# Another order for weight conversions, sums and copies in an attention and two-layer kernel

## The chip, the core and the metric

The kernel runs on one core of one Trainium2 chip. The time is that of the whole program on the device in microseconds (us). PE is TensorE (matrix products), DVE is VectorE, ACT is ScalarE, POOL is GpSimd, SP is SyncE, which here only issues DMAs. Every engine works through its own queue in order: an instruction that waits holds up all that stand behind it on that engine.

## The reference

```python
# attention with a decay per head, for 2 sequences of 768, 8 heads of 64
for t in range(S):
    state = gamma[None, :, None, None] * state + np.einsum('bhd,bhe->bhde', k[:, :, t], v[:, :, t])
    y[:, :, t] = scale * np.einsum('bhd,bhde->bhe', q[:, :, t], state)
...
x = np.ascontiguousarray(attn_out.transpose(0, 2, 1, 3)).reshape(B * S, H * D)   # 1536 x 512
...
return (a * b @ w_out)      # a = x @ w_a, b = x @ w_b; d_ff 1536: the first layer, gives y
...
h = x @ w_in                # the second layer, x is y; d_ff 2048
g = np.maximum(0.01 * h, h)
return (g @ w_out)
```

## The kernel before

**Numbers.** Every product runs with two-part operands: a value is rounded to a short form, `hi`, by ACT, and the rest, `lo`, is the difference, taken by DVE (`split`). A product is three matmuls, hi·hi, hi·lo and lo·hi (`mm3`, L249 to L251). The weights come from HBM in 64 bits a number (`raw`). They are brought to 32 bits, which the code calls rounding: `begin_weights` issues three ACT instructions (absolute value, low bits, sign) and `round_steps` three DVE instructions (L309, L311, L315). Then a weight is split like any other operand.

**Stages on PE.** Attention runs 0 to 47 us in 12 units `u` (256-column pieces of scores, states and outputs). The first layer follows in 12 blocks of `d_ff`, f = 0 to 11, to 246 us: `a` and `b` are products of x with weight blocks a_f and b_f, their product is h[t, f] for the three 512-token tiles t. From f = 3 to 10 (`fast`) the block uses sums of x made beforehand (`mixed_items`: eight DVE sums `xf`, L675, and eight splits s, L683) to save products. Then comes y's stage, 248 to 326 us: h times w_out by Strassen's scheme of seven products, each over six j (class `Seven`; its n = 6 to 41 here, `blk` in the trace, one product of 2.1 us for each n, in the order p7, p2, p6, p5, p4, p3). For every n it makes operand forms (`forma`): an ACT cast and a DVE difference for each part of h and w_out. They are prepared four products ahead (`LEAD1`). The second layer's h2 = y · w_in follows with f = 0 to 15 (326 to 490 us), with the products `blk<-form` of its own w_out in between, and its tail runs to 580 us.

**What sets the order.** The order on every engine is the order in which the code is run. A list `queue` holds small items with a cost in us; `pump(us)` runs items while PE's work of that length is emitted. `enqueue_round` and `enqueue_split` put a weight's rounding and split on it; two tables, `PARK` and `WITH`, say which further weights are rounded in which f: `WITH` the blocks of w_out (wo), `PARK` first blocks of the second layer's wi and wq, which are stored to HBM (L321, POOL's queue) and fetched again.

**Space.** SBUF has 81 slots of 128x512 numbers. A new tile takes the slot that was given back longest ago, and waits for the last user of it. Of h's blocks 18 (`AWAY`) are sent to HBM as soon as they are made (`send`, L650, POOL's queue) and brought back (`bring`, L660, SP's queue). The sums of h that the seven products need are accumulating DMAs in POOL's queue (L127); some read the sent block in HBM. For a brought block h[2, f] with f < 6 `bring` also issues an accumulating DMA (L662), an add-back, which waits for the bring.

Of the kernel before, what the change touches and what calls it, by code (L numbers as in the profile page):

```python
# [14 lines left out]
U32 = mybir.dt.uint32  # L15
I64 = mybir.dt.int64
ALU = mybir.AluOpType
# [17 lines left out]
LATE = 8  # L35
STEPS = {6: 1, 7: 1, 8: 1, 9: 1, 10: 1}
NWARM = 10
# [4 lines left out]
LEAD1 = 4  # L42
PARK = (0, 0, 0, 0, 0, 0, 0, 0, 0, 0, 1, 2)
WITH = ((), (), (), (0,), (1,), (2,), (3,), (4,), (5,), (6, 7), (8, 9), (10, 11))
MADE = ((), (), (), (), (0,), (1,), (2,), (3,), (4,), (5,), (), ())
# [176 lines left out]
def retention_moe_kernel(ctx: ExitStack, tc: tile.TileContext, ins, out):  # L222
# [61 lines left out]

    def begin_weights():

        n = at["begin"]
        key = order[n]
        raw = raws[key]
        u = slots.new(F32, f"{key[0]}{key[1]}")  # L290
        low = tmp.tile([P, TT], I32, tag="low", name=f"low{n}")
        nc.scalar.activation(u, word(raw, F32, 1), AF.Abs, scale=2.0 ** -112)
        nc.scalar.mul(low, word(raw, U32, 0), 2.0 ** -29)
        sign = signs[n % len(signs)]
        nc.scalar.mul(word16(sign, F16, 1), word(raw, F32, 1), 2.0 ** -100)
        begun[key] = (u, low, sign)
        at["begin"] += 1
# [61 lines left out]
    def enqueue_split(key, keep=False):  # L359
# [4 lines left out]
        def low():  # L364
            src = rounded.pop(key)
            if key[0] == "a":
                nc.scalar.mul(weights[key][1], as32(weights[key][0]), -1.0)
                nc.gpsimd.dma_start(weights[key][1], src, accum_op=ALU.add)
            else:
                nc.vector.tensor_sub(weights[key][1], src, as32(weights[key][0]))  # L370
            if keep:
                kept[key] = src
            else:
                slots.done(1)

        behind.extend([(0.05, high), (0.05 if key[0] == "a" else 0.61, low)])

# [265 lines left out]

    far = {}

# [8 lines left out]
    def bring(reserve=0):  # L654

        for key in list(far)[:1]:
# [4 lines left out]
            if key[0] == 2 and key[1] < FF1 // 2:  # L661
                nc.gpsimd.dma_start(h[key], h[2, key[1] + FF1 // 2], accum_op=ALU.add)  # L662

# [136 lines left out]
    for i in range(2):  # L800
        signs.append(tmp.tile([P, TT], I32, tag=f"sign{i}", name=f"sign{i}", bufs=1))
        nc.gpsimd.memset(signs[i], 0)
    warm = ap.tile([P, TT], BF16, tag="warm", name="warm")
# [15 lines left out]
    def first_weights():  # L819
        begin_weights()  # L820
        yield
        yield from round_steps()
        yield
        want("a", 0)
# [3 lines left out]
    for u in range(-1, len(units)):  # L828
# [21 lines left out]
        if u < 0:  # L850
            prep(2)
        else:
            prep(u + 3)
        loads(u + 8)
        if u + 8 == 7 or u + 8 >= len(units):
# [17 lines left out]
    for t in range(NTILE):  # L873
        if t < 2:
            want("ab"[t], 1)
        pbs.append(bank(f"pb{t}0"))
        ab_mm(pbs[t], t, 0, 1, range(KC))
# [28 lines left out]
    for f in range(1, FF1):  # L906
        if f + 1 < FF1:
            for k in "ab":
                enqueue_round()
                enqueue_split((k, f + 1), f + 1 in FAST)  # L910
        for n in MADE[f][:1]:
# [74 lines left out]
    for n in range(NMADE, len(z.plan) - 2):  # L986
        bring(8)
        if n == NMADE:
            bring(8)
        z.prep(n + LEAD1)  # L990
        if n >= 3 * H1:
# [9 lines left out]
        if n == 6 * H1 - LEAD1:  # L1001
            slots.done(H1)
        if n in (5 * H1, 6 * H1 - 2):
            want("wi", int(n != 5 * H1))
# [75 lines left out]
    for f in range(FF2):  # L1080
# [4 lines left out]
        for n, step in enumerate(steps):  # L1085
# [4 lines left out]
            if n == 0 and f == FF2 - 1:  # L1090
                keep(z, u2, "p1")
            if n == 0 and f >= HALF:
                z.prep(f)
            if n == (f > 0):
                if f + 1 < FF2:
# [91 lines left out]
```

## Time and profile before

| what | value |
|---|---|
| median of 3 runs | 582.33 us (581.12 to 582.61) |
| the profiled execution | 582.3 us, of which 580.4 us are the span of instructions |
| busy: PE, DVE, ACT, POOL | 570.8, 448.0, 374.3, 85.6 us |
| granted TensorE clock | 1.00 of full speed throughout |

The span is what the profile shows from the first to the last instruction; 1.9 us of the execution lie outside it. PE's busy time is 98% of the span, and PE's instructions and their order are the same before and after the change.

### The profile page before, as it was taken

The numbers are of one execution on the slowest core, as the hardware profiler recorded it, in microseconds if no ns is written. First come the engines' busy times: TensorE is split into PE (matmuls) and PEld (weight loads), VectorE is DVE, ScalarE is ACT, GpSimd is POOL, SyncE is SP. The second block draws the span as 40 slices with busy tenths as digits, with TensorE's granted clock in tenths as the row PEclk, the third lists the DMA queues.
The fourth block names the chain that finished last, engine by engine and source line by source line (L and its number), as shares of the span: only waits on it lengthen the run. The fifth ranks groups of instructions, "written<-read, shape, count | busy, mean of one in ns | idle before, by whom it ended". The sixth has DMA issues, their size and how long they took to land.

```text
span 580.4 us, 9183 instructions
## 1 busy us (share of the span) xinstructions
PE 570.8 (98%) x3287; PEld 479.8 (83%) x3287; DVE 448.0 (77%) x899; ACT 374.3 (64%) x778; POOL 85.6 (15%) x107
## 2 busy tenths in 40 slices
PE   9999989999999999999999999999999999999997
PEld 5988878888888887888788878888888888888886
DVE  5886497898897985796799487676887657879992
ACT  4776456776676865784768487767675456688710
POOL 3331300013233211038900000000000000000000
PEclk9999999999999999999999999999999999999999
DMA  8994923557676565699960052433431000010111
GB/s 326 386 365 167 238 86 96 158 140 170 172 209 188 157 204 185 244 331 196 189 139 1 0 182 78 141 108 110 142 98 51 1 0 1 2 55 1 56 54 55
DMA packets 34702, 79.59 MB, mean 137 GB/s; under 512 B 4000, under 2 KB 8352, under 8 KB 34656
## 3 DMA queue, kind: packets, MB, share of 16 engines
q1 hardware_dynamic: 23184, 58.99, 29.7%
q0 software_dynamic: 11184, 19.67, 17.2%
q8 instruction: 26, 0.43, 0.3%
q10 hardware_dynamic: 288, 0.34, 0.2%
q14 instruction: 20, 0.16, 0.1%
HBM read 57.49 MB, written 8.65 MB: 114 GB/s over the span
## 4 chain that ended last, share of the span: by engine, by line
PE 82%; DMA 8%; issue 3%; DVE 3%; ACT 2%; POOL 1%; DVEq 0%; POOLq 0%; ACTq 0%
PE blk L250 10%; PE blk L249 10%; PE blk L251 10%; PE h L251 8%; PE h L249 8%; PE h L250 8%; DMA h<-far 3%; PE sc L503 2%; PE top L249 2%; PE top L250 2%; PE top L251 2%; DMA xf<-x02l 2%; PE pa L251 2%; PE pb L251 2%; PE pb L249 2%
## 5 line engine op out<-in xcount | busy, mean ns | idle before, releaser
L250 PE MATMUL blk<-form,form 128*128 128x512 f32 (+1 forms) x224 | 75.8, 338 | 0.0
L249 PE MATMUL blk<-form,form 128*128 128x512 f32 (+1 forms) x224 | 75.5, 337 | 0.0
L251 PE MATMUL blk<-form,form 128*128 128x512 f32 (+1 forms) x224 | 75.3, 336 | 0.0
L157 DVE TENSOR_TENSOR form<-g,form 128x512 fp32r<-128x512 f32 x112 | 57.2, 551 | 2.4 <-ACT form L151 0.7
L1039 ACT ACTIVATE g<-h 128x512 f32<-128x512 f32 x48 | 28.6, 596 | 46.3 <-PE h L251 46.3
L151 ACT CAST form<-g 128x512 fp32r<-128x512 f32 x112 | 52.7, 514 | 8.5 <-DVE g L132 6.4
L249 PE MATMUL blk<-forma,forma 128*128 128x512 f32 (+1 forms) x168 | 56.8, 338 | 1.0 <-ACT forma L151 1.0
L250 PE MATMUL blk<-forma,forma 128*128 128x512 f32 (+1 forms) x168 | 57.1, 340 | 0.3 <-DVE forma L157 0.2
L251 PE MATMUL blk<-forma,forma 128*128 128x512 f32 (+1 forms) x168 | 56.5, 336 | 0.0
L157 DVE TENSOR_TENSOR forma<-h,forma 128x512 fp32r<-128x512 f32 x84 | 42.9, 550 | 8.7 <-ACT forma L151 8.2
L249 PEld LDWEIGHTS blk<-form,form 128*128 128x128 f32 x224 | 42.5, 190 | 5.5
L250 PEld LDWEIGHTS blk<-form,form 128*128 128x128 f32 x224 | 42.5, 190 | 5.0
L251 PEld LDWEIGHTS blk<-form,form 128*128 128x128 f32 x224 | 42.3, 189 | 4.7
L151 ACT CAST forma<-h 128x512 fp32r<-128x512 f32 x84 | 39.2, 511 | 8.7 <-DMA h<-far 6.6
L127 POOL DMA_DIRECT2D h<-h x34 | 36.2, 1409 | 5.2 <-DVE forma L157 2.7
L157 DVE TENSOR_TENSOR form<-wq,form 128x256 fp32r<-128x256 f32 x56 | 23.5, 419 | 17.1 <-ACT form L151 16.6
L249 PEld LDWEIGHTS blk<-forma,forma 128*128 128x128 f32 x168 | 31.9, 190 | 5.1 <-ACT forma L151 1.2
L250 PEld LDWEIGHTS blk<-forma,forma 128*128 128x128 f32 x168 | 31.8, 190 | 4.5 <-DVE forma L157 0.9
L251 PEld LDWEIGHTS blk<-forma,forma 128*128 128x128 f32 x168 | 31.7, 189 | 3.4
L132 DVE TENSOR_TENSOR g<-g,g 128x512 f32<-128x512 f32 (+1 forms) x56 | 30.6, 570 | 0.5 <-ACT g L1039 0.5
L151 ACT CAST form<-wq 128x256 fp32r<-128x256 f32 x56 | 22.6, 404 | 5.4 <-PE blk L251 2.1
L650 POOL DMA_DIRECT2D far<-h x18 | 10.1, 563 | 89.6 <-DVE h L740 45.0
(3081 smaller groups left out, 1565.9 us busy)
## 6 DMA issues: line engine op xcount, KB each, us to landing
raw_wi<-in_w SPq DMA_DIRECT2D x16, 512.0 KB, 3.4
raw_wq<-in_w SPq DMA_DIRECT2D x16, 512.0 KB, 3.4
raw_a<-in_wab SPq DMA_DIRECT2D x12, 512.0 KB, 5.5
raw_b<-in_wab SPq DMA_DIRECT2D x12, 512.0 KB, 4.0
raw_wo<-in_wo SPq DMA_DIRECT2D x12, 512.0 KB, 5.1
far<-h POOLq DMA_DIRECT2D x18, 256.0 KB, 4.5
h<-far SPq DMA_DIRECT2D x18, 256.0 KB, 6.6
h<-far POOLq DMA_DIRECT2D x13, 256.0 KB, 7.0
```

The lines of the kernel that those rows point to most:

```text
L127: queue.append((0.0, lambda piece=piece: self.nc.gpsimd.dma_start(self.A(*d[1:], j)[piece], self.A(*x1[1:], j)[piece], accum_op=ALU.add)))
L132: queue.append((cost, lambda piece=piece: run(*(self.A(*x[1:], j)[piece] for x in (d, x0, x1)))))
L151: nc.scalar.copy(h, src)
L157: nc.vector.tensor_sub(*todo.pop(0))
L249: nc.tensor.matmul(ps, w[0], x[0], start=first, stop=False, skip_group_check=more)
L250: nc.tensor.matmul(ps, w[0], x[1], start=False, stop=False, skip_group_check=more)
L251: nc.tensor.matmul(ps, w[1], x[0], start=False, stop=last, skip_group_check=more)
L503: nc.tensor.matmul(sc[h][:, c], d["k"][r, c], d["qs"][r, c], start=True, stop=True)
L650: nc.gpsimd.dma_start(far[t, f], h[t, f])
L1039: nc.scalar.activation(g[t, f], ps, AF.Lrelu, alpha=0.01)
```

## The change

It changes order only, with two small exceptions: the `lo` parts of two weights (a2 and a11) are made another way, and one weight less (wi1) is stored and fetched.

- **Third weight blocks.** a2 and b2 are put on the list while f = 0 is still running, ahead of the x sums, where they stood after them before. a2's and a11's `lo` is made by a DVE difference in place of an ACT negation and an accumulating DMA on POOL's queue (L367, L368).
- **Tables.** One stored weight less (wi1), and wo7 is rounded in the list of f = 10 in place of f = 9.
- **h's sums.** The blocks h[2, f] are brought back from n = 12 on, not from n = 6 on, and their three add-backs are issued together at n = 16, behind the 21 sums of p7.
- **w_in roundings.** wi1 and wq1 are rounded in y's stage, on the list of n = 13 and n = 24; wi2 is then split at f = 0, n = 2 of the second layer.
- **Late splits.** For f = 11 to 14 of the second layer the ACT part of the next wi's rounding stands right after the first step's `g`.
- **Begin.** The three ACT instructions of a rounding are ordered absolute, sign, low (before: absolute, low, sign), and for a0 in attention they are spread over units 6 and 7. The two clears of the sign buffers go from POOL's start to units 3 and 4.

```diff
-STEPS = {6: 1, 7: 1, 8: 1, 9: 1, 10: 1}
+STEPS = {6: 2, 7: 2, 8: 1, 9: 1, 10: 1}
...
-PARK = (0, 0, 0, 0, 0, 0, 0, 0, 0, 0, 1, 2)
-WITH = ((), (), (), (0,), (1,), (2,), (3,), (4,), (5,), (6, 7), (8, 9), (10, 11))
+PARK = (0, 0, 0, 0, 0, 0, 0, 0, 0, 0, 0, 2)
+WITH = ((), (), (), (0,), (1,), (2,), (3,), (4,), (5,), (6,), (7, 8, 9), (10, 11))
...
     def begin_weights():
+        for _ in begin_steps():
+            pass
+
+    def begin_steps():
...
         nc.scalar.activation(u, word(raw, F32, 1), AF.Abs, scale=2.0 ** -112)
-        nc.scalar.mul(low, word(raw, U32, 0), 2.0 ** -29)
+        yield
         sign = signs[n % len(signs)]
         nc.scalar.mul(word16(sign, F16, 1), word(raw, F32, 1), 2.0 ** -100)
+        yield
+        nc.scalar.mul(low, word(raw, U32, 0), 2.0 ** -29)
...
-            if key[0] == "a":
+            if key[0] == "a" and keep:
                 nc.scalar.mul(weights[key][1], as32(weights[key][0]), -1.0)
                 nc.gpsimd.dma_start(weights[key][1], src, accum_op=ALU.add)
...
+    def enqueue_next(f):
+        for k in "ab":
+            enqueue_round()
+            enqueue_split((k, f), f in FAST)
...
             if key[0] == 2 and key[1] < FF1 // 2:
-                nc.gpsimd.dma_start(h[key], h[2, key[1] + FF1 // 2], accum_op=ALU.add)
+                back.append(key)
+
+    def add_back():
+        for _, f in back:
+            nc.gpsimd.dma_start(h[2, f], h[2, f + FF1 // 2], accum_op=ALU.add)
+        back.clear()
...
-        nc.gpsimd.memset(signs[i], 0)
...
+        if u in (3, 4):
+            nc.gpsimd.memset(signs[u - 3], 0)
...
     for t in range(NTILE):
         if t < 2:
             want("ab"[t], 1)
+        if t == 1:
+            enqueue_next(2)
+            queue.extend(behind)
+            behind.clear()
...
     for f in range(1, FF1):
-        if f + 1 < FF1:
-            for k in "ab":
-                enqueue_round()
-                enqueue_split((k, f + 1), f + 1 in FAST)
+        if 1 < f < FF1 - 1:
+            enqueue_next(f + 1)
...
     for n in range(NMADE, len(z.plan) - 2):
-        bring(8)
-        if n == NMADE:
+        if n >= 2 * H1:
             bring(8)
+        if n == 3 * H1 - 2:
+            add_back()
...
+        if n in (2 * H1 + 1, 4 * H1):
+            enqueue_round()
...
+            if n == 0 and f >= FF2 - 5 and at["begin"] < min(at["load"], len(order)):
+                begin_weights()
             if n == 0 and f >= HALF:
                 z.prep(f)
+            if f == 0 and n == 2:
+                want("wi", 2)
```

On DVE, where f = 1 begins, this stood before (xf20 is the sum of x for tile 2, part 0; a2_145 the weight a2 in slot 145, and the last number of a name counts tiles):

```order
L675 TENSOR_TENSOR xf22_129_888<-xf20_127_882,xf22_129_888 128x512
L675 TENSOR_TENSOR xf20_127_882<-xf00_131_894,xf20_127_882 128x512
L675 TENSOR_TENSOR xf00_131_894<-xf22_129_888,xf00_131_894 128x512
L675 TENSOR_TENSOR xf02_133_900<-xf02_133_900,xf00_131_894 128x512
L626 TENSOR_TENSOR h20_143_1020<-h20_143_1020,pb20_1007 128x512
L675 TENSOR_TENSOR xf23_130_891<-xf21_128_885,xf23_130_891 128x512
L675 TENSOR_TENSOR xf21_128_885<-xf01_132_897,xf21_128_885 128x512
L675 TENSOR_TENSOR xf01_132_897<-xf23_130_891,xf01_132_897 128x512
L675 TENSOR_TENSOR xf03_134_903<-xf03_134_903,xf01_132_897 128x512
L309 TENSOR_SCALAR a2_145_1043<-a2_145_1043 128x512
L311 SCALAR_TENSOR_TENSOR a2_145_1043<-a2_145_1043,sign0_90 128x512
L315 ISA a2_145_1043<-a2_145_1043,low4_1044 128x1024
```

and this stands there now:

```order
L315 TENSOR_SCALAR a2_143_1003<-a2_143_1003 128x512
L317 SCALAR_TENSOR_TENSOR a2_143_1003<-a2_143_1003,sign0_90 128x512
L321 ISA a2_143_1003<-a2_143_1003,low4_1004 128x1024
L637 TENSOR_TENSOR h20_145_1031<-h20_145_1031,pb20_1018 128x512
L315 TENSOR_SCALAR b2_144_1013<-b2_144_1013 128x512
L376 TENSOR_TENSOR a2l_147_1036<-a2_143_1003,a2h_146_1035 128x512
L317 SCALAR_TENSOR_TENSOR b2_144_1013<-b2_144_1013,sign1_91 128x512
L321 ISA b2_144_1013<-b2_144_1013,low5_1014 128x1024
L376 TENSOR_TENSOR b2l_150_1060<-b2_144_1013,b2h_149_1059 128x512
L691 TENSOR_TENSOR xf22_129_888<-xf20_127_882,xf22_129_888 128x512
L691 TENSOR_TENSOR xf20_127_882<-xf00_131_894,xf20_127_882 128x512
L691 TENSOR_TENSOR xf00_131_894<-xf22_129_888,xf00_131_894 128x512
```

The roundings of a2 and b2 moved ahead of all x sums, and the product into h20 ahead of b2's rounding; the `lo` of both (L376) also stands ahead of the sums.

On POOL, from the last stores of the first layer on, this stood before (h23 is h[2, 3]; far29 the sent h[2, 9] in HBM; L321 stores, L662 adds back, L127 sums):

```order
L321 DMA wq0_2719<-wq0_312_2694 128x512
L321 DMA wi1_2765<-wi1_313_2721 128x512
L662 DMA h23_329_2814<-far29_2459 128x512
L662 DMA h24_330_2817<-far210_2598 128x512
L127 DMA h00_138_969<-far26_1945 128x512
L127 DMA h10_142_999<-h16_305_2662 128x256
L127 DMA h20_143_1020<-far26_1945 128x512
L127 DMA h10_142_999<-h16_305_2662 128x256
L127 DMA h01_144_1041<-far27_2113 128x512
L662 DMA h25_333_2851<-h211_318_2750 128x512
L127 DMA h11_151_1099<-h17_307_2666 128x256
L127 DMA h21_168_1161<-far27_2113 128x512
```

and this stands there now:

```order
L327 DMA wi0_2705<-wi0_311_2680 128x512
L327 DMA wq0_2751<-wq0_312_2707 128x512
L127 DMA h00_138_969<-far26_1944 128x512
L127 DMA h10_142_999<-h16_304_2648 128x256
L127 DMA h20_145_1031<-far26_1944 128x512
L127 DMA h10_142_999<-h16_304_2648 128x256
```

The first sum now follows the second store. The end of p7's sums and what follows them now reads:

```order
L127 DMA h14_198_1427<-h110_325_2786 128x256 x2
L127 DMA h05_212_1575<-h211_317_2736 128x512
L127 DMA h15_213_1576<-h111_310_2674 128x256 x2
L677 DMA h23_343_2972<-far29_2448 128x512
L677 DMA h24_346_2996<-far210_2584 128x512
L677 DMA h25_350_3027<-h211_317_2736 128x512
L127 DMA h06_303_2646<-h00_138_969 128x512
L127 DMA h16_304_2648<-h10_142_999 128x256
```

The three add-backs (L677 now) moved from among the first six sums to behind the 21 sums of p7; x2 marks two alike.

On ACT, in f = 10, between the split of a11 and the first copy out of the bank `top10` (h010, h210 and u10 are copied out of that bank one after the other), this stood before:

```order
L362 CAST a11h_293_2467<-a11_291_2436 128x512
L367 ACTIVATE a11l_294_2468<-a11h_293_2467 128x512
L292 ACTIVATE wo8_295_2476<-raw_wo8_2351 128x512
L293 ACTIVATE low32_2477<-raw_wo8_2351 128x512
L295 ACTIVATE sign0_90<-raw_wo8_2351 128x512
L362 CAST b11h_296_2498<-b11_292_2452 128x512
L292 ACTIVATE wo9_298_2506<-raw_wo9_2392 128x512
L293 ACTIVATE low33_2507<-raw_wo9_2392 128x512
L295 ACTIVATE sign1_92<-raw_wo9_2392 128x512
L707 COPY h010_288_2426<-top10_2511 128x512
L292 ACTIVATE wi0_299_2531<-raw_wi0_2450 128x512
```

and this stands there now:

```order
L368 CAST a11h_292_2456<-a11_290_2425 128x512
L296 ACTIVATE wo7_294_2480<-raw_wo7_2295 128x512
L299 ACTIVATE sign1_91<-raw_wo7_2295 128x512
L301 ACTIVATE low31_2481<-raw_wo7_2295 128x512
L368 CAST b11h_295_2486<-b11_291_2441 128x512
L723 COPY h010_287_2415<-top10_2490 128x512
L296 ACTIVATE wo8_297_2509<-raw_wo8_2350 128x512
L299 ACTIVATE sign0_90<-raw_wo8_2350 128x512
L301 ACTIVATE low32_2510<-raw_wo8_2350 128x512
L630 COPY h110_288_2416<-pa10_2418 128x256
L632 ACTIVATE h110_288_2416<-pa10_2418 128x256
L736 COPY u10_298_2531<-top10_2490 128x512
```

One rounding less (wo9's, and wi0's behind it, went later) stands ahead of h010's copy, and the negation a11l is gone.

## Rows read from the trace of the kernel before

**Rows 1.** The page, span and part 1: busy us, share, instructions.

```profile
span 580.4 us, 9183 instructions
...
PE 570.8 (98%) x3287; PEld 479.8 (83%) x3287; DVE 448.0 (77%) x899; ACT 374.3 (64%) x778; POOL 85.6 (15%) x107
```

**Rows 2.** PE's waits: us in total, times, longest.

```profile
PE pa L251 <- DMA a2l<-a: 1.8, 1, 1.8
...
PE blk L249 <- ACT forma L151: 1.0, 1, 1.0
```

**Rows 3.** DVE's timeline, 66 to 78: start, us, instruction, [idle before <- releaser].

```profile
66.42 0.69 DVE L675 TENSOR_TENSOR xf<-xf,xf 128x512 f32<-128x512 f32 x1 [3.34 <-DMA xf<-x22l]
...
75.58 0.42 DVE L309 TENSOR_SCALAR a<-a 128x512 f32<-128x512 f32 x1
...
76.83 0.69 DVE L315 CUSTOM_DVE_ANT_0 a<-a,low 128x1024 uint16<-128x1024 uint16 x1
```

**Rows 4.** PE's timeline, 80 to 83.

```profile
80.28 0.39 PE L250 MATMUL pa<-x00l,a2h 128*128 128x512 f32 x1
82.46 0.50 PE L251 MATMUL pa<-x00h,a2l 128*128 128x512 f32 x1 [1.79 <-DMA a2l<-a]
82.79 0.40 PE L249 MATMUL pa<-x01h,a2h 128*128 128x512 f32 x1
```

**Rows 5.** PE's timeline, 222.

```profile
222.40 0.50 PE L249 MATMUL top<-s20h,tb10h 128*128 128x512 f32 x1 [1.00 <-ACT h L707]
```

**Rows 6.** The chain that ended last: start us, us, what.

```profile
214.96 6.72 DMA far<-h
...
270.44 8.42 DMA h<-far
```

**Rows 7.** POOL's timeline, 217.

```profile
217.61 0.56 POOL L650 DMA_DIRECT2D far<-h  x1 [1.17 <-DVE h L745]
```

**Rows 8.** ACT's timeline, 228.

```profile
228.21 0.59 ACT L726 COPY h<-top 128x512 f32<-128x512 f32 x1 [2.31 <-PE top L251]
```

**Rows 9.** PE's timeline, 283 to 284.

```profile
283.37 0.49 PE L249 MATMUL blk<-forma,forma 128*128 128x512 f32 x1 [0.96 <-ACT forma L151]
284.10 0.50 PE L250 MATMUL blk<-forma,forma 128*128 128x512 f32 x1 [0.23 <-DVE forma L157]
```

**Rows 10.** POOL's timeline, 249 to 259.

```profile
249.26 0.54 POOL L321 DMA_DIRECT2D wi<-wi  x1 [3.59 <-DVE wi L315]
256.89 1.80 POOL L662 DMA_DIRECT2D h<-far  x2 [7.08 <-DMA h<-far]
258.12 1.47 POOL L127 DMA_DIRECT2D h<-far  x1
```

**Rows 11.** Windows: engines' busy us (x), PEclk, DMA share, GB/s.

```profile
270.00:285.00 15.00, 13.79 (x75) 11.40 (x75) 7.09 (x17) 6.89 (x17) 12.53 (x16) 1.00 1.17 196
300.00:320.00 20.00, 20.00 (x118) 17.60 (x117) 20.00 (x44) 14.26 (x35) 0.00 (x0) 1.00 0.01 4
```

**Rows 12.** DVE's timeline, 290.

```profile
290.06 0.42 DVE L157 TENSOR_TENSOR forma<-wo,forma 128x256 fp32r<-128x256 f32 x1
```

**Rows 13.** PE's timeline, 345 to 346.

```profile
345.40 0.50 PE L249 MATMUL h<-y000h,wi2h 128*128 128x512 f32 x1 [0.87 <-ACT wi2h L243]
345.73 0.40 PE L250 MATMUL h<-y000l,wi2h 128*128 128x512 f32 x1
346.12 0.50 PE L251 MATMUL h<-y000h,wi2l 128*128 128x512 f32 x1
```

**Rows 14.** PE's timeline, 448 to 449.

```profile
448.67 0.40 PE L250 MATMUL h<-y000l,wi12h 128*128 128x512 f32 x1
449.07 0.50 PE L251 MATMUL h<-y000h,wi12l 128*128 128x512 f32 x1
```

**Rows 15.** PE's timeline, 30 and 33.

```profile
30.76 0.82 PE L596 MATMUL xp<-qs,wk 128*64 128x128 f32 x12
...
33.90 1.29 PE L596 MATMUL xp<-qs,wk 128*64 128x128 f32 x12
```

More of the change, by code (lines that the diff above doesn't have):

```diff
@@ L374, in low @@
                 slots.done(1)
-        behind.extend([(0.05, high), (0.05 if key[0] == "a" else 0.61, low)])
+        behind.extend([(0.05, high), (0.05 if key[0] == "a" and keep else 0.61, low)])
+    def enqueue_next(f):
+        for k in "ab":
+            enqueue_round()
+            enqueue_split((k, f), f in FAST)
     kept = {}
@@ L641, in ab_step @@
         pump(2.05)
-    far = {}
+    far, back = {}, []
     def send(t, f):
@@ L819, in first_weights @@
     def first_weights():
-        begin_weights()
+        yield from begin_steps()
         yield
```

## The prediction

> **What bounds the kernel now.** I read the page first: PE is busy 570.8 of a span of 580.4 us [rows 1], with the same instructions in the same order before and after. So the change can only win the time that PE stands, or lose by new standing time. Second, PE's waits: they are few, single and each has a name [rows 2]. Third, PE's timeline around each: the price of a wait is not the idle time in brackets, since a matmul's end is modelled, but the distance between two starts. In [rows 4] 80.28 to 82.46 is 2.18 us, and a 512-column matmul behind a 128x512 one normally starts 0.23 us later; the next step (82.46 to 82.79) is still 0.10 too long. So a wait shown as 1.79 costs 1.95 + 0.10 = 2.05 us. I add the same 0.26 to the brackets of the other stalls. Last, for each wait, the timeline of the engine that ends it and the chain that ended last, to see what that engine had been waiting for in its turn.
>
> **The change part by part**, against the profiled execution (582.3 us, of which 1.9 lie outside the span; the median of the runs is 582.33, so the two need no conversion).
>
> *A, third weight blocks.* PE waits for a2's low part at 82.46 [rows 4]. DVE could not round a2 before 75.58 because the x sums stood ahead, and the first of these waited 3.34 us for a transfer [rows 3]. The rounding takes from 75.58 to 77.52 (its third instruction starts at 76.83 and takes 0.69); then came the ACT cast, the negation and an accumulating DMA. Now the rounding stands where DVE idled, the DMA is gone, and the low part costs one more DVE instruction of 0.69. Two roundings and two low parts are 2 x 1.94 + 2 x 0.69 = 5.3 us; begun at the start of that idle time (63.1) they end at 68.4, and some us later would still be ahead of 80.28. They push the x sums back by 5.3 less the 3.3 of idle time, so these end near 77.5 where they ended at 75.58, and the splits for f = 3 stay ahead of f = 3's own a3, whose rounding follows them as before but without a2's and b2's 3.9 in between. Saving: 2.05.
>
> *B, f = 10.* PE waits at 222.40 for the copy of h010 [rows 5], and that copy waits for its slot, which the send of h29 held from 214.96 for 6.72 us [rows 6]. With one rounding less in front, the slot handed to h010 is another, free one, and the slots of sends fall to u10 (h29's) and h210 (h09's). The send of h09 was issued at 217.61 [rows 7]; with 6.72 us it lands at 224.3. h210's copy stood at 228.21 [rows 8], that is 226.95 without the stall: 2.6 us of cover. The send of h29 has landed at 221.7, before even h010 is copied in the trace; u10's copy comes after that one. Saving: 1.00 + 0.26 = 1.26; if the cover were gone, it would be paid again.
>
> *C, y's stage.* PE waits at 283.37 and at 284.10 for forms [rows 9]. The chain goes back from there: the accumulating DMA that finishes h03 took from 270.44 to 278.86 [rows 6], one of 21 in POOL's queue that could start only at 258.12, because the add-back at 256.89 waited 7.08 us for h23 to be brought [rows 10]. Now the sums stand directly behind the second store, which was at 249.26 [rows 10], and h23 is brought later. If h03's sum lands as long after the first sum as before (278.86 - 258.12 = 20.7 us), it lands at 270.0, 8.9 us earlier, where 2 would do. Cover for the later add-backs: the forms that use h23 were made at 290.06 [rows 12], and the add-backs, at the DMA rate of 196 GB/s [rows 11], follow 21 sums (9 of 0.262 MB and 12 of 0.131, 3.9 MB: 20.1 us) and take 4.0 themselves, and one needs 8.4 to land [rows 6]: 249.3 + 20.1 + 4.0 + 8.4 = 281.8. Saving: 0.96 + 0.23 + 2 x 0.26 = 1.71. Bounds: nothing, if the sums are held up as long as before, and 2.0, if the small delays just before 283 go as well.
>
> *The skill's rule here.* The row: with sums alone in the air the DMA engines are 1.17 busy at 196 GB/s [rows 11]. The Trainium skill (DMA: Bandwidth & Descriptors, "Issuing engines are not separate DMA queues") says that transfers issued by different engines run on the same 16 DMA engines and interleave. By that rule the brings, now issued while sums run, slow them, and C may bring nothing; no run here shows the two at that place yet. It is the first rival.
>
> *The roundings of wi1 and wq1* put 2 x 1.94 = 3.9 us on DVE in y's stage, which is full from 300 to 320 (20.00 of 20.00 [rows 11]). What covers it: from 270 to 285 DVE was busy 7.09 of 15 us, because forms waited for sums. If these come 8.9 us sooner, DVE starts its full stretch sooner by more than the 3.9. Cost: nothing; without that cover up to 3.9.
>
> *D, wi2.* PE waits for wi2's high part (345.40) and then for its low part (345.73 to 346.12 is 0.39) [rows 13]. Two roundings less stand before wi2's, so it is split 3.9 us sooner, where 1.4 would do. Saving: 0.87 + 0.26 + 0.16 + 0.10 = 1.39. The work is covered by y's stage, as above.
>
> *E, the last four wi.* From 448.67 to 449.07 PE takes 0.40 for a step of 0.23, as wi12's low part is late, and 0.10 behind it [rows 14]: 0.27, which I take for each of the four. The ACT part now stands one step earlier and the sign, for which DVE waited, comes before the low bits. Saving: 4 x 0.27 = 1.08; at worst nothing, since the forms that the ACT part delays have room.
>
> *F, attention.* The 12 matmuls at 33.90 take 1.29 where those at 30.76 take 0.82 [rows 15]: ACT's three instructions for a0 stand ahead of the copies that feed them. Spread over two units, two of them are still there, but shorter in sum. Saving: 0.47, at worst nothing.
>
> The clears of the sign buffers lie between POOL's products, where it has time: nothing.
>
> Sum: 2.05 + 1.26 + 1.71 + 1.39 + 1.08 + 0.47 = 7.96. Time: 582.3 - 8.0 = **574.3 us**.
>
> **The rivals.**
>
> *1. The sums stay late* (C gives nothing). For it: the rate above, and eight brings of 0.262 MB, at 196 GB/s 10.7 us, enter the same stretch. Against: they are issued from n = 12 on, after most of the sums that p2's forms wait for. Then DVE has no cover, and part of the 3.9 us is seen too; half of it is 1.9. Time: 582.3 - 8.0 + 1.7 to 1.7 + 1.9, so 576.0 to 577.9.
>
> *2. A stall moves instead of going.* B's to h210 or u10, if a send takes 2.6 us longer than 6.72: 574.3 + 1.3 = 575.6. A's to f = 3, if the x sums' transfers come still later than in [rows 3] because the next weights are loaded sooner: 574.3 + 2.05 = 576.4. Against both: the covers above.
>
> *3. Slower: the add-backs come too late.* Place: POOL's queue behind p7's 21 sums, where the add-back of h23 waits for its bring, and the twelve sums behind it wait too. If sums and brings share the rate, the add-backs land at 281.8 + 10.7 = 292.5, 2.4 us after 290.06, and ACT, which waits in order, holds up all later forms as well. Each us of lateness is one for PE. C is then lost too, so 6.3 us remain to be used up, and slower by more than 0.3% (1.75 us, about what a measurement of this kernel can tell from no change) begins when they land 8 us late, at 298. For it: nothing but the sum of all upper bounds. Time at 8 us: 584.
>
> *4. The change doesn't do what it says,* each removed wait being followed by another just behind it: PE's other inputs at these places (b2, the next forms) are late as well. In [rows 9] that is what happens (0.96 and then 0.23). If half the sum is kept: 578.3; if under a fifth: no change.
>
> **How the numbers follow.** Chances: forecast, to within 1.3 us, 0.50; rival 1 0.17; rival 2 0.14; rival 4 with half 0.08, with less than a fifth 0.06; rival 3 0.05. The predicted time is that of the first, 574.3. The range for 8 in 10 reaches down by 1.3 (0.3 for the small delays left out in C, and 1.0 of the 1.2 us by which the fastest run lies under the median), to 573.0, and up to the end of rival 1, 577.9; outside lie most of rival 4 and rival 3. Faster by over 0.3% (under 580.6): 0.50 + 0.17 + 0.14 + 0.08 = 0.89; same 0.06; slower 0.05.
>
> **What would show it.** PE's waits lose pa, top, blk and h; 0.23 us steps stand at the places of [rows 4, 5, 9, 13, 14]. POOL's first sum starts near 246 (all earlier parts' savings taken off 249) and nothing waits 7 us there; the waits of ACT's form casts for sums are gone. DVE from 285 to 320 is full, with two roundings among the forms, and PE doesn't wait for it. The forecast is wrong if PE waits for a form of p5 or p4 (n = 24 to 35), for s splits at f = 3, or for u10 or h210 at f = 10.

## The result and the profile after

The changed kernel takes 574.49 us (median of 4 runs, 574.40 to 575.24) against 582.47 (581.12 to 583.47): ratio 0.9867, 95% interval 0.9846 to 0.9889, so 1.3% faster. Forecast were 574.3 us and a saving of 8.0. The profiled execution took 574.53 us with a span of 572.8, which is 7.6 less than before. The kernel before ran 32 times more beside the experiments: in 23 of these runs its mean granted clock was 0.996 or 0.997 and the median 582.6 us, in the other nine 0.999 or 1.00 and 580.9, so a part of the 8.0 us between the medians may lie in the executions; what lowers that clock no trace here shows.

The page after, with the span and part 1 as in [rows 1]:

```profile
span 572.8 us, 9199 instructions
...
PE 567.5 (99%) x3287; PEld 479.8 (84%) x3287; DVE 447.8 (78%) x901; ACT 371.9 (65%) x776; POOL 82.7 (14%) x104
```

PE has the same instructions and loses standing time. (Its busy time falls by 3.3 us all the same, from 570.8 to 567.5, because the ends of matmuls are modelled and a part of each late start counts as busy.) Its waits in the changed kernel (us in total, times, longest) are the start's and nothing else:

```profile
PE warm L828 <- DVE warm L819: 1.2, 1, 1.2
PE sc L514 <- DVE qs L496: 0.2, 1, 0.2
```

All waits of [rows 2] are gone. The starts tell the same: at a2 the steps are 0.23 where [rows 4] had 2.18 and 0.33, at wi2 0.23 to 0.24 where [rows 13] had 0.33 and 0.39, at wi12 0.23 to 0.24 where [rows 14] had 0.40. PE's timeline at the three places:

```profile
79.80 0.39 PE L250 MATMUL pa<-x00l,a2h 128*128 128x512 f32 x1
80.03 0.39 PE L251 MATMUL pa<-x00h,a2l 128*128 128x512 f32 x1
80.25 0.39 PE L249 MATMUL pa<-x01h,a2h 128*128 128x512 f32 x1
...
339.11 0.40 PE L249 MATMUL h<-y000h,wi2h 128*128 128x512 f32 x1
339.35 0.40 PE L250 MATMUL h<-y000l,wi2h 128*128 128x512 f32 x1
339.58 0.39 PE L251 MATMUL h<-y000h,wi2l 128*128 128x512 f32 x1
...
441.95 0.40 PE L250 MATMUL h<-y000l,wi12h 128*128 128x512 f32 x1
442.18 0.39 PE L251 MATMUL h<-y000h,wi12l 128*128 128x512 f32 x1
```

In attention the 12 matmuls after u = 6 take 0.88 where [rows 15] had 1.29. In f = 10 PE takes up the bank `top10` without a wait, and both parts of the form of [rows 9] are there in time:

```profile
33.84 0.88 PE L607 MATMUL xp<-qs,wk 128*64 128x128 f32 x12
...
218.49 0.39 PE L251 MATMUL pa<-x13h,a10l 128*128 128x512 f32 x1
218.71 0.39 PE L249 MATMUL top<-s20h,tb10h 128*128 128x512 f32 x1
...
278.15 0.40 PE L249 MATMUL blk<-forma,forma 128*128 128x512 f32 x1
278.38 0.40 PE L250 MATMUL blk<-forma,forma 128*128 128x512 f32 x1
```

In y's stage POOL starts the sums right behind the second store, at 245.93, and the 7.08 us wait of [rows 10] is gone; h03's sum is issued at 259.14 and lands at 266.46, 12.4 us earlier than before. The add-backs come at 268.92. POOL's timeline:

```profile
245.40 0.54 POOL L327 DMA_DIRECT2D wq<-wq  x1 [3.96 <-DVE wq L321]
245.93 0.93 POOL L127 DMA_DIRECT2D h<-far  x1
...
259.14 0.86 POOL L127 DMA_DIRECT2D h<-far  x1 [0.72 <-DVE wo L121]
...
268.92 1.83 POOL L677 DMA_DIRECT2D h<-far  x2 [1.32 <-PE blk L251]
```

But the stage is not free of delays. PE's timeline there has two steps of 0.42 and 0.43 with 0.34 and 0.33 behind them where 0.23 is normal, 0.3 each and 0.6 us in all, at the forms of n = 28 and 29 (p5). They are too small for the list of PE's waits. The first stands here; that of n = 29 is at 293.15 to 293.91:

```profile
290.75 0.39 PE L249 MATMUL blk<-forma,forma 128*128 128x512 f32 x1
291.17 0.50 PE L250 MATMUL blk<-forma,forma 128*128 128x512 f32 x1
291.51 0.39 PE L251 MATMUL blk<-forma,forma 128*128 128x512 f32 x1
```

DVE's timeline shows what came late: form 27's differences wait 2.45 us, then come six instructions on `up`, and form 28's long differences run from 290.43 to 291.45, when PE has begun that form at 290.75 and wants the `lo` parts 0.23 later; the first two rounding steps of wq1 (the second at 291.89) stand between forms 28 and 29.

```profile
285.18 1.03 DVE L157 TENSOR_TENSOR forma<-h,forma 128x512 fp32r<-128x512 f32 x2 [2.45 <-ACT forma L151]
...
290.43 1.02 DVE L157 TENSOR_TENSOR forma<-h,forma 128x512 fp32r<-128x512 f32 x2
```

And ACT, which releases DVE, waits for sums at three places (forms 23 and 27, and wq1's first instruction, which takes a slot that a sum still reads):

```profile
276.18 0.62 ACT L151 CAST forma<-h 128x512 fp32r<-128x512 f32 x1 [2.68 <-DMA h<-h]
...
283.13 0.93 ACT L151 CAST forma<-h 128x512 fp32r<-128x512 f32 x2 [1.63 <-DMA h<-h]
...
287.05 0.68 ACT L296 ACTIVATE wq<-raw_wq 128x512 f32<-128x512 f32 x1 [1.86 <-DMA h<-h]
```

So the forecast that "the waits of ACT's form casts for sums are gone" failed: before they were 6.6 + 1.9 us from 262 to 292, now they are 4.9, later and nearly harmless. In the windows, the DMA engines move 256 GB/s at a share of 1.14 where the five last brings and the load of a raw weight (`raw_wi`, at 262.50) run among the sums (262 to 277), and 208 at 1.16 without them (277 to 292; same columns as [rows 11]):

```profile
262.00:277.00 15.00, 15.00 (x87) 13.12 (x87) 11.93 (x28) 9.07 (x22) 9.63 (x12) 1.00 1.14 256
277.00:292.00 15.00, 14.97 (x86) 12.90 (x85) 12.05 (x26) 11.14 (x28) 8.30 (x10) 1.00 1.16 208
```

The share doesn't rise when SP's queue sends beside POOL's. The Trainium skill (DMA: Bandwidth & Descriptors, "Issuing engines are not separate DMA queues") says that transfers issued by different engines run on the same 16 DMA engines and interleave. The trace agrees as far as the share goes (1.14 with both queues, 1.16 with POOL's alone). From a first sum at 245.93 the terms of the prediction have the three add-backs landed by 278.4 (245.93 + 20.1 + 4.0 + 8.4); they landed at 279.25, 280.58 and 281.83, the last 3.4 us later, as sharing would have it.

### The profile page after: what moved, and what is told of

It is laid out like the page before. It is cut to its first block, busy times and chain, and to the rows that moved or that the text cites. A ratio compares the mean times of both kernels' runs of the same rounds, so it can differ in the third digit from the quotient of the medians.

```text
span 572.8 us, 9199 instructions
## 1 busy us (share of the span) xinstructions
PE 567.5 (99%) x3287; PEld 479.8 (84%) x3287; DVE 447.8 (78%) x901; ACT 371.9 (65%) x776; POOL 82.7 (14%) x104
## 4 chain that ended last, share of the span: by engine, by line
PE 99%; DVE 0%; issue 0%
PE blk L250 12%; PE blk L249 12%; PE blk L251 12%; PE h L250 8%; PE h L249 8%; PE h L251 8%; PE pa L249 3%; PE pa L250 3%; PE pb L250 3%; PE pa L251 3%; PE pb L251 3%; PE pb L249 3%; PE top L249 3%; PE top L250 3%; PE top L251 3%; PE sc L514 2%
## 5 line engine op out<-in xcount | busy, mean ns | idle before, releaser
L127 POOL DMA_DIRECT2D h<-h x34 | 34.0, 1102 | 8.1 <-DVE forma L157 4.1
```

Of the source, the lines that this page charges most:

```text
L127: queue.append((0.0, lambda piece=piece: self.nc.gpsimd.dma_start(self.A(*d[1:], j)[piece], self.A(*x1[1:], j)[piece], accum_op=ALU.add)))
```

## The experiments

All start from the changed kernel; "as before" means the old form of one part. PE's instructions and their order are the same in all. Each time is a median of 4 to 8 executions, one of them profiled. Runs of one kernel differ by 0.5 to 1.7 us, in three kernels by 2 to 4, so for parts of less than a microsecond the profile's steps decide, and the times only support them. The changed kernel's 574.49 was not measured again beside the experiments; the kernel before was, and its median was 583.17 for experiments 1 to 4, 582.51 for 5 to 8 and 582.46 for 9 to 12, against 582.47 with the result. So up to 0.7 us between a time below and 574.49 can come from the occasion.

**1. Sums as before, roundings kept.**

```diff
-                back.append(key)
+                nc.gpsimd.dma_start(h[key], h[2, key[1] + FF1 // 2], accum_op=ALU.add)
...
-        if n >= 2 * H1:
+        bring(8)
+        if n == NMADE:
             bring(8)
-        if n == 3 * H1 - 2:
-            add_back()
```

> The changed kernel with brings from n = 6 and add-backs issued with each bring again, all else as changed (the roundings of wi1 and wq1 stay in y's stage). My sum (C worth 1.71 by itself): 574.5 + 1.7 = 576.2, with PE waiting near the form of n = 22 again. Rival (C's early sums were also DVE's cover for the two roundings, 3.9 us): more than 1.7, up to 574.5 + 1.7 + 3.9 = 580.1, with further PE waits for forms of p5 (n = 27 to 30). Rival (early sums bought nothing since brings and sums share the DMA engines): 574.5, no new wait.

Measured: 578.61 us (577.51 to 579.14), 4.1 above the changed kernel's median; the profiled execution was the fastest of the five, 577.51. POOL waits for the bring again, as its timeline shows, and PE at the forms of n = 21 and 22, as in its timeline behind it:

```profile
253.51 1.79 POOL L673 DMA_DIRECT2D h<-far  x2 [6.70 <-DMA h<-far]
```

PE's timeline, the same run:

```profile
277.84 0.50 PE L250 MATMUL blk<-forma,forma 128*128 128x512 f32 x1 [0.23 <-DVE forma L157]
...
280.99 0.49 PE L249 MATMUL blk<-forma,forma 128*128 128x512 f32 x1 [1.02 <-ACT forma L151]
...
281.72 0.50 PE L250 MATMUL blk<-forma,forma 128*128 128x512 f32 x1 [0.23 <-DVE forma L157]
```

PE's excess at these two forms, against the same steps of the changed kernel, sums to 2.6 us in this profile, where C was put at 1.71, at most 2.0. There is no PE wait at the forms of n = 27 to 30, and the 0.6 us at n = 28 and 29 are gone. So the early sums are what removed C's stall; brings and sums in the air together did not cancel that. In this profile PE ends 2.8 us later than in the changed kernel's: 2.6 at C, less the 0.6, and 0.9 in attention and at f = 4, where nothing was changed. By the ratios to the kernel before (0.9909 against 0.9867) the two kernels lie 2.4 us apart, so a part of the 4.1 may be the occasion.

**2. Roundings as before** (no rounding of wi1 and wq1 in y's stage, wi2 split late).

```diff
-        if n in (2 * H1 + 1, 4 * H1):
-            enqueue_round()
...
-            if f == 0 and n == 2:
-                want("wi", 2)
```

> The changed kernel without the two roundings in y's stage and without the early split of wi2. My sum: D comes back, 1.39, PE waits for wi2's high part again: 574.5 + 1.4 = 575.9. If the two small new delays of PE in y's stage (0.33 each, at the forms of n = 28 and 29) come from wq1's rounding on DVE, one or both go, and the total is 575.2 to 575.6 with steps of 0.23 there. If they come from forms that wait for sums, they stay: 575.9.

Measured: 576.08 us (575.25 to 576.58). D is back as priced, with steps as in [rows 13]:

```profile
340.04 0.50 PE L249 MATMUL h<-y000h,wi2h 128*128 128x512 f32 x1 [0.87 <-ACT wi2h L243]
340.37 0.40 PE L250 MATMUL h<-y000l,wi2h 128*128 128x512 f32 x1
340.76 0.50 PE L251 MATMUL h<-y000h,wi2l 128*128 128x512 f32 x1
```

The two delays at n = 28 and 29 are gone. In the profiles PE ends 1.3 us later than in the changed kernel: 1.4 of D, less these 0.6, and 0.5 at f = 3 and f = 4, where nothing was changed. By the ratios to the kernel before (0.9867 both) the times show no difference, so D's price rests on the steps.

**3. Both as before.** The two diffs above together.

> Both of the former edits together: sums as before and no roundings in y's stage. If C and D are independent: the two prices of the former runs added (1.7 + 1.4: 577.6). If C's early sums are the cover for the roundings: less than the sum of the two, since without the roundings no cover is needed; then the run with sums alone as before is about as slow as this one or slower.

Measured: 578.08 us (577.09 to 580.47), by the times the same as experiment 1 (ratios to the kernel before 0.9916 and 0.9909) although D's 1.39 us are paid again. In the profile, C's excess is 0.9 in place of 2.6, and the end of the stage has a new wait of 0.68. So, when sums are late, C's stall is 1.7 us longer with wi1's rounding than without. It was sized at 3.9 at most. That DVE's time is the reason is not shown: in experiment 1 DVE stands idle, 4.61 and 2.56 us, right in front of the late forms. What differs besides is that the rounding frees the buffer of a raw weight, and SP loads the next, 512 KB, at 263.34 (landed at 271.88); without the rounding no such load stands there. SP's timeline and then DVE's, experiment 1:

```profile
263.34 0.33 SPq L275 DMA_DIRECT2D raw_wi<-in_w  x1
```

```profile
273.17 1.03 DVE L157 TENSOR_TENSOR forma<-h,forma 128x512 fp32r<-128x512 f32 x2 [4.61 <-ACT forma L151]
```

Two sums in flight then take 9.51 and 9.96 us from issue to landing, and the same two 8.17 and 7.98 in experiment 3. So the load among the sums is the likelier cause; no run keeps the rounding and leaves out the load.

**4. Five brings later.**

```diff
-        if n >= 2 * H1:
+        if 2 * H1 <= n < 2 * H1 + 3 or n >= 3 * H1 + 2:
             bring(8)
```

> The changed kernel with the last five of the eight brings (h[2, 6] to h[2, 10]) issued from n = 20 on in place of n = 15 on. In the changed kernel they run from 263 to 278 us among the sums, and sums take 8 to 11 us to land there. If brings and sums share the DMA engines (first rival of the prediction, in part true): the sums behind land 3 to 4 us sooner (five times 0.26 MB at the 256 GB/s of that stretch is 5 us), ACT's waits for sums at 283 and 287 go, and so do PE's two delays of 0.33: 574.5 - 0.65 = 573.8. If the delays come from wq1's rounding on DVE alone: they stay, 574.5. If the brings are now too late for p4's forms: PE waits for a form of n = 30 or later.

Measured: 574.05 us (573.77 to 574.61). From 262 to 292 ACT's waits of form casts for sums fall from 4.9 to 2.9 us, the wait of form 27 at 283 is gone, and PE's two delays with it. ACT's waits in that stretch:

```profile
ACT forma L151 <- DMA h<-h: 2.9, 4, 1.8
ACT wq L296 <- DMA h<-h: 2.8, 1, 2.8
```

wq1's wait (2.8) stays, so that wait alone did not make PE late. p4's forms are not late. But the sum that form 27 waited for does not land sooner: p2's first sum lands at 283.10 in the changed kernel, where the cast starts at 283.13, and at 283.29 here, where the cast starts 1.7 us ahead of it. So the cast has another slot, since a bring takes slots too. ACT's timeline, this run:

```profile
281.62 0.92 ACT L151 CAST forma<-h 128x512 fp32r<-128x512 f32 x2
```

The run shows that the place of the brings matters for the delays; it does not show that their share of the DMA engines does.

**5. a2's rounding behind the x sums again,** its low part still by DVE.

```diff
-        if t == 1:
-            enqueue_next(2)
-            queue.extend(behind)
-            behind.clear()
...
-        if 1 < f < FF1 - 1:
+        if f < FF1 - 1:
             enqueue_next(f + 1)
```

> The changed kernel with a2's and b2's roundings behind the x sums again; the low part of a2 still by a DVE difference. If the place of the rounding is what PE's wait for a2 came from: +2.05, 576.5. If the place and the way of the low part each suffice (the rounding ended at 77.5 before, a cast and a difference of 0.6 and 0.7 us would be done near 80, PE wants it at 80.5): 0 to 0.5 more, 574.5 to 575.0.

Measured: 578.80 us (577.38 to 581.13), 4.3 slower than the changed kernel: both expectations missed. PE does not wait for a2 (its steps there are 0.23), but it waits at f = 3 and the blocks after it. PE's timeline, from the profiled execution, the slowest of the six:

```profile
102.97 0.50 PE L249 MATMUL top<-s20h,tb3h 128*128 128x512 f32 x1 [1.38 <-ACT h L723]
...
111.30 0.50 PE L251 MATMUL pa<-x10h,a4l 128*128 128x512 f32 x1 [0.38 <-DMA a4l<-a]
...
114.33 0.51 PE L249 MATMUL top<-x22h,ta3h 128*128 128x512 f32 x1 [1.83 <-ACT h L742]
```

The first of these waits is for a3's chain: the copy of h03 stands at 102.34 where the changed kernel has it at 98.96 and the kernel before at 101.50, and PE wants its bank at about 101.4 here, at 101.3 in the changed kernel and only at 103.9 before. The other two stand behind a4's accumulating DMA, which took 6.88 us in this execution, and 5.0 in both the kernel before and the changed one.

The clock falls too. In the windows, PE is busy 9.68 of 12 us, then not at all for 1.30; then the granted clock is 0.56, with 512-column steps of 0.42 to 0.43, the lower of its two levels (1.2 GHz), until 118; from 118 to 125 it is 0.99 again:

```profile
101.00:113.00 12.00, 9.68 (x39) 6.71 (x37) 7.75 (x14) 6.71 (x14) 0.90 (x1) 1.00 0.54 155
113.00:114.30 1.30, 0.00 (x0) 0.00 (x0) 1.08 (x3) 1.30 (x4) 0.00 (x0) 1.00 0.00 0
114.30:118.00 3.70, 3.67 (x9) 2.91 (x10) 3.46 (x7) 3.70 (x7) 0.00 (x0) 0.56 0.25 75
```

By the steps the fall cost about 1.6 us (an estimate: eight steps longer by 0.2). It is not what makes this kernel slower: three of its six executions have a mean granted clock of 1.00 and took 577.74, 578.59 and 579.0 us.

**6. a2's low part by DMA again,** the rounding's place kept. The item's cost on the list goes with it, from 0.61 back to 0.05, as it does in experiment 9; in 12 it goes from 0.05 to 0.61.

```diff
-            if key[0] == "a" and keep:
+            if key[0] == "a" and (keep or key[1] == 2):
```

> The changed kernel with a2's low part by negation and accumulating DMA again; the rounding stays ahead of the x sums. With the rounding done near 65 and a DMA of 3.3 us, the low part lands ten us before PE wants it: no change, 574.5. Rival (POOL's queue, where eight accumulating DMAs for x stand and their transfers are under way, holds it up): up to 2.05 more.

Measured: 575.00 us (574.67 to 575.25), and PE's steps at a2 are 0.23. In y's stage the delays are 0.8 in this profile (0.6 in the changed kernel's). So the place of the rounding is enough for A, and the DMA costs nothing there. At a2 itself the DVE difference alone is enough too (experiment 5), but then the wait moves to f = 3.

**7. wo7 as before.**

```diff
-WITH = (..., (5,), (6,), (7, 8, 9), (10, 11))
+WITH = (..., (5,), (6, 7), (8, 9), (10, 11))
```

> The changed kernel with wo7 rounded in the list of f = 9 again; a11's low part stays on DVE and the parked weights stay two. If the place of wo7's rounding decides which slot h010 gets: PE waits for h010's copy again, 1.26 or less as the send may start sooner now, 575.0 to 575.8. If the weight less on the list or the missing DMA for a11 decides: no wait, 574.5.

Measured: 575.65 us (574.56 to 575.75), no wait at f = 10; PE lost 0.72 at f = 4, before anything that was edited, where DVE waited 1.41 us for a5's accumulating DMA, and 1.0 in y's stage. The copy of h010 starts at 217.28, before h29's send has landed (217.90), so it has another slot.

**8. Add-backs later.**

```diff
-        if n == 3 * H1 - 2:
+        if n == 3 * H1 + 4:
             add_back()
```

> The changed kernel with the three add-backs issued at n = 22, behind the first two of p2's twelve sums (0.39 MB, near 2 us of transfer), the latest place before the form that uses them. If add-backs are what the forms of n = 27 to 29 wait for (third rival): PE's delays there grow by 1.5 to 2 us, 576.0 to 576.5. If those forms wait for p2's first sums, whose source slots they take: these now come 3 add-backs sooner, and the delays shrink or stay, 573.8 to 574.5.

Measured: 574.00 us (573.64 to 574.20), no delay of PE in y's stage. So the forms of n = 27 to 29 did not wait for the add-backs but for p2's first sums, whose source slots they take; with these ahead of the add-backs, issued at 269.55 in place of 273.29 and landed at 279.31, the delays go. The third rival's mechanism is absent here.

**9. wo7 as before and a11's low part by DMA.** The diff of experiment 7, and:

```diff
-            if key[0] == "a" and keep:
+            if key[0] == "a" and (keep or key[1] == 11):
```

> The changed kernel with both wo7 rounded in the list of f = 9 and a11's low part by negation and accumulating DMA again; the parked weights stay two. With wo7 alone as before PE did not wait at f = 10, h010 took a free slot. If the slot order is made by both together (each takes or returns one slot): h010 is handed h29's slot again, PE waits for its copy 1.0 to 1.3 us: 575.5 to 575.8. If the third parked weight is what decided: no wait at f = 10, 574.5.

Measured: 576.04 us (575.20 to 576.46). B's stall is back: PE waits 1.17 by the bracket, 1.43 with the 0.26 that brackets lack. Behind it stands the send of h29 again, 6.79 us long, near the 6.72 of [rows 6]. a11's accumulating DMA is issued right behind it (213.06 to 220.60 here), as in the kernel before; without that DMA the send takes 4.62 us in the changed kernel and 4.65 in experiment 7. A send of 4.65 would have landed at 217.15, before ACT comes to the copy at 218.36 (an estimate from these rows), and nothing would have waited.

PE's timeline:

```profile
220.01 0.50 PE L249 MATMUL top<-s20h,tb10h 128*128 128x512 f32 x1 [1.17 <-ACT h L723]
```

ACT's timeline, the copy that PE waits for:

```profile
219.37 0.58 ACT L723 COPY h<-top 128x512 f32<-128x512 f32 x1 [1.01 <-DMA far<-h]
```

The chain that ended last (start us, us, what):

```profile
212.50 6.79 DMA far<-h
```

**10. Brings and add-backs later,** the diffs of 4 and 8.

> The changed kernel with both the five later brings issued from n = 20 on and the add-backs issued at n = 22. Each alone took away PE's two delays of 0.33 in y's stage. If these delays were all that was left there: both together give the same as each, 573.8 to 574.1. If the transfers still set the pace of the stage: a little less again, 573.5.

Measured: 574.59 us (573.66 to 575.34, six runs). The profiled execution (573.77) has no delay in y's stage, but the times are no better than the changed kernel's. Experiments 4 and 8 are 0.4 to 0.5 us below the changed kernel in the median; with this run beside them, a gain is shown in the profile's steps, not in the time.

**11. Late begin and attention as before.**

```diff
-STEPS = {6: 2, 7: 2, 8: 1, 9: 1, 10: 1}
+STEPS = {6: 1, 7: 1, 8: 1, 9: 1, 10: 1}
...
     def first_weights():
-        yield from begin_steps()
+        begin_weights()
...
-            if n == 0 and f >= FF2 - 5 and at["begin"] < min(at["load"], len(order)):
-                begin_weights()
```

> The changed kernel with the ACT part of the late wi roundings not moved ahead, and with a0's ACT part in one piece at u = 6; the order absolute, sign, low stays. F: +0.47, the 12 matmuls after u = 6 take 1.3 again in place of 0.8. E: if the earlier place of the ACT part is what saves (my E), +1.08; if the new order of the three alone makes the low part early enough (the sign is there 0.6 us sooner, PE's delay was 0.27), 0. Total 574.5 + 0.5 to 1.55: 575.0 to 576.1.

Measured: 575.70 us (575.12 to 576.66). The 12 matmuls after u = 6 take 1.18, and 0.83 a unit earlier, which looks as if F were back. But the same matmuls take 0.82 to 1.09 in seven of the other experiments, 1.27 in experiment 1 and 1.29 in experiments 4, 5 and 7, all of which keep the change in attention. So F changes from execution to execution, and neither its saving nor its return is shown. PE's timeline in experiment 4:

```profile
34.09 1.29 PE L607 MATMUL xp<-qs,wk 128*64 128x128 f32 x12
```

E is not back: at wi12 the steps stay 0.23 and 0.24. PE's timeline, this run:

```profile
34.63 1.18 PE L607 MATMUL xp<-qs,wk 128*64 128x128 f32 x12
...
443.21 0.40 PE L250 MATMUL h<-y000l,wi12h 128*128 128x512 f32 x1
443.45 0.39 PE L251 MATMUL h<-y000h,wi12l 128*128 128x512 f32 x1
```

The sign's part shows in DVE's second rounding instruction, which waits for it: 0.81 us at wi12 in the kernel before, 0.25 here. DVE's timeline, the kernel before and then this run:

```profile
446.21 0.69 DVE L311 SCALAR_TENSOR_TENSOR wi<-wi,sign 128x512 int32<-128x512 int32 x1 [0.81 <-ACT sign L295]
```

```profile
440.24 0.69 DVE L317 SCALAR_TENSOR_TENSOR wi<-wi,sign 128x512 int32<-128x512 int32 x1 [0.25 <-ACT sign L299]
```

So the new order of the three ACT instructions was enough for E, and the earlier place bought nothing more. Whether the earlier place alone would do was not tried.

**12. a2's rounding behind the x sums, and a3's low part by DVE.** The diff of experiment 5, and:

```diff
-            if key[0] == "a" and keep:
+            if key[0] == "a" and keep and key[1] != 3:
```

> The run in which a2's rounding stands behind the x sums again, with one thing more: a3's low part by a DVE difference in place of the accumulating DMA, which took 3.97 us from issue to landing there, and for which DVE's differences for f = 3 (they overwrite a3) waited 2.1 us. In that run PE did not wait for a2 but for the copies of h03 and h23 out of their banks, which stand in ACT's queue behind casts that wait for those differences. If that chain (a3's rounding, its DMA, the differences, the casts) is what A's wait moved to: the wait at f = 3 (1.55) shrinks below 0.5, that at the next f (2.0) at least by half, and the time falls from 578.8 to 576 or less. If the copies wait for slots or banks: no change, 578 to 579.

Measured: 576.03 us (575.17 to 577.34), 2.8 less than experiment 5. PE's wait for h03's copy at f = 3 is gone; that for h23's copy is 0.55 in place of 1.83, and the clock holds. The wait for h23's copy owes a part to the execution: a4's accumulating DMA, which stands behind it, took 4.73 us here and 6.88 in experiment 5. By the ratios to the kernel before (0.9894, interval 0.9867 to 0.9920, against 0.9940, 0.9922 to 0.9958) the gain is there all the same:

```profile
110.57 0.50 PE L249 MATMUL top<-x22h,ta3h 128*128 128x512 f32 x1 [0.55 <-ACT h L742]
```

## Why the prediction held, point by point

**The bound.** Only PE's standing time moved, as forecast. Matched start by start between the two profiles, PE gains 2.06 at A, 1.27 at B, 2.01 at C (0.28 of it in the small delays that the forecast left out), 1.40 at D, 1.07 at E and 0.44 at F; it loses 0.60 at n = 28 and 29; about 0.4 is in small drifts elsewhere. Its last matmul starts 8.0 us earlier. The span falls by only 7.7 because 3.8 us run behind that matmul where 3.4 did before, for which the profiles give no cause. So the terms were right one by one, but that the time came out within 0.2 us is luck: the 0.28, the 0.60, the drifts and the end were not in the sum and nearly cancel.

**A (2.05): right in size.** The step "DVE could not round a2 before the x sums" is confirmed by experiment 6, where only the rounding's place was new. No run puts the place and the DMA back together, so A's price is read from the steps (2.06). What my working missed is that the stall at a2 sheltered f = 3. With a2's low part early and the rest late (experiment 5), PE arrives at f = 3 2.4 us sooner than before and finds a3's chain 0.8 us later, where it had 1.8 us to spare: rounding, accumulating DMA, differences, casts, and behind these in ACT's queue the copies out of PE's banks. Taking a3's DMA out of that chain removes the wait for h03's copy (experiment 12); the longer wait, for h23's, hangs on a4's DMA as well, which was slow in that execution. The second rival ("A's to f = 3") is therefore real; in the changed kernel it does not occur since a3's rounding starts at 84.85 on DVE where it started at 87.61 before. My forecast had that step (the splits and a3 without a2's and b2's 3.9 us between them), but as a side remark, not as what the saving hangs on.

**B (1.26): right in size (1.43 in experiment 9), the step half wrong.** I had it from "one rounding less in front". With that rounding put back alone (experiment 7) h010 still takes a free slot. With the DMA for a11 put back as well (experiment 9) it is handed h29's slot again. That DMA counts in a second way, which my working did not have: it makes the send of h29 itself last 6.8 us in place of 4.6. What the DMA alone would do was not tried. The third parked weight was not needed for the stall; what its return alone would do was not tried either.

**C (1.71): the mechanism right, the remainder mis-sized.** The stall is gone with the early sums (2.01 with the small delays) and back with late ones: 2.6 in experiment 1, 0.9 in experiment 3, so its size depends on what runs beside them. Two points failed: sums still hold up casts, and PE is late by 0.6 at forms of p5 (n = 28 and 29), which the forecast had named as a sign of being wrong; it is small, but it is there. These delays go when the brings are later (4), when p2's sums come sooner (8), when the roundings are not there (2), and also with the sums as before (1, 3); they are 0.6 to 1.1 in the other runs. In the changed kernel, form 27's cast has the slot that p2's first sum still reads; with later brings it has another. The first rival's sharing of the DMA engines fits the add-backs, which landed 3.4 us later than the forecast's terms give. What it costs PE is not shown apart from the slots; in the changed kernel it is 0.6 at most.

**The two roundings (cost nothing): nearly right.** With early sums they cost at most the 0.6 (experiment 2). With late sums C's stall is 1.7 us longer with them than without (1 against 3). This is the sign that the forecast gave for a missing cover of DVE's time, but DVE stood idle in front of those forms; the load of a raw weight that the rounding sets off is the likelier cause, and is untested.

**D (1.39) right; E (1.08) right in size, with the order of the ACT instructions enough; F (0.47) not shown.** The profile of the changed kernel has 0.41 of F, but four experiments that keep F's change show none of it (1.27 to 1.29 where the kernel before has 1.29), so its 0.41 in the forecast's favour is luck of the profiled execution.

**Rival 4** (another wait right behind) did not occur.

## What to carry to other kernels

When a wait is removed, look at the next block's inputs: the time that the wait gave them is gone as well, and half a remedy can cost more than none, as the early low part of a2 without the early rounding did. A slot pool hands out slots in the order of their return, so one allocation more or less can give or take a wait on a transfer far from the edit; read who used the slot last. Where the parts of a change are below a run's spread, the distance between PE's starts at the place tells what the times can't; but look at the same place in other runs that keep the part, since one profile can show a saving that the next one lacks, as F did.

## What was not expected of the hardware

After stalls that left PE 9.68 of 12 us busy and then 1.30 us idle, the granted clock was 0.56 for 3.7 us (experiment 5), so the stalls were dearer than their own length, by about 1.6 us as estimated there. The accumulating DMA of one 128x512 weight part took 3.99 us at a3 in that run, from its issue at 91.93 until the waiting DVE instruction started at 95.92, and 6.88 at a4 (104.40 to 111.28), where the kernel before had 3.7 and 5.0, and the waits at f = 3 and 4 in kernels that are alike up to there differ by up to 0.7 us between executions. The send of one 128x512 block took 6.7 to 6.8 us with an accumulating DMA issued right behind it (the kernel before and experiment 9) and 4.6 without (the changed kernel and experiment 7).
